# Loading one input in 640-byte runs by four narrow loads, with heads paired g and g+4, in a chunked linear-attention kernel

## The chip, the cores and the metric

One core of one Trainium2 chip (the sets of runs were taken on several chips, each with the kernel before in the same rounds). The metric is device microseconds of one execution. A time quoted below is the median of all runs of a kernel, of which up to two are marked slow (over 1.5% above its fastest run); a ratio is of fast runs alone.

The engines go by their short names: PE is TensorE (matmuls and transposes), ACT ScalarE, DVE VectorE, POOL GpSimd. SP is SyncE, which here computes nothing and issues DMA transfers; SPq is its queue. To issue a load is the instruction that starts it; the 16 DMA engines then move it in packets, one for each contiguous run. An eviction copies a result of PE out of its accumulation buffer. The chain of waits is followed back from the last instruction: at each step to what it had waited for.

## The reference

An RWKV-7-like recurrence, then a mixing layer. Only the first part touches the change.

```python
# r, k, v, w, a, b: (batch 4, heads 8, seq 768, head_dim 40), float32
for t in range(S):
    y[:, :, t] = einsum('bhd,bhde->bhe', rt, state)
    Sa = einsum('bhde,bhe->bhd', state, at)
    state = state * wt[:, :, None, :] - einsum('bhd,bhe->bhde', Sa, bt) + einsum('bhd,bhe->bhde', vt, kt)
# then x = y as (batch, seq, 320):  theta = x @ w_theta;  y = w_tok_r @ (x cos theta) + w_tok_i @ (x sin theta)
# u = x + y;  out = u + relu(u @ w_ch)
```

## The kernel before

The sequence is cut in 24 tiles of 128 time steps (6 for each batch entry). For a tile the six inputs are loaded with time on the partitions: each partition gets 8 heads x 40 floats, which lie 8 x 160 bytes apart in memory, so one 160 KB load is 1024 runs of 160 bytes. Pairs of heads are then transposed on PE and evicted by ACT.

```python
def load(i):                                    # cut: r and v share a buffer
    def src(ap):
        return ap[bi, :, ci * C:(ci + 1) * C, :].rearrange("h t d -> t h d")
    return (..., (("raw_r", s), raw_rv[s][:, 0], src(r)),
                 (("raw_v", s), raw_rv[s][:, 1], src(v)))

def loads(i):
    for key, dst, src in load(i):
        add("SP", "load", i, lambda dst=dst, src=src: nc.sync.dma_start(out=dst, in_=src),
            650, [], [key], work=1030)
...
# in prep(i): r and v copied to bf16 (POOL), 8 transposes (PE), one eviction (ACT)
tr("trv", "erv", (rv[:, 0], rv[:, 1]), rvT_t[i % (NTR + 1)], ...)
```

`add` does not emit at once. It records an operation with an estimated cost, and a planner then fixes the order of all operations on every engine from these costs and from priorities (`OFF`, `TIMES`), found by search. Each engine runs its list strictly in that order. All loads go through SP's queue. For them the planner keeps one clock of DMA work, and lets SP run ahead of it by a fixed time:

```python
SP_DEPTH = 3600.0
te = max(te, dma - SP_DEPTH)            # SP may issue when DMA work ahead is under 3.6 us
free[o.eng] = t + o.cost                # then SP is busy for `cost` ...
dma = max(dma, t + 1350.0) + o.work     # ... and the DMA engines for `work`
```

## Time and profile before

| | before |
|---|---|
| time, median of the first 4 runs | 219.81 us (219.03 to 221.12) |
| PE busy | 197.0 us of a span of 217.5 us |
| DVE, ACT, POOL busy | 166.0, 146.9, 118.4 us |
| loads: packets of 160 bytes | 147,456 of 155,684 |

From the page of the kernel before: PE's busy row of part 1; busy tenths in 40 slices of the span; DMA packets; the main queue; the chain of waits.

```profile
span 217.5 us, 8118 instructions
...
PE 197.0 (91%) x3368; PEld 155.8 (72%) x3368; DVE 166.0 (76%) x250; ACT 146.9 (68%) x319; POOL 118.4 (54%) x184
...
PE   1487898888898899999999999999999999999993
...
PEclk9999999999999999999999999999999999999999
DMA  6998989989998999999978999899897010101022
...
DMA packets 155684, 30.81 MB, mean 142 GB/s; under 512 B 150400, under 2 KB 155648, under 8 KB 155648
...
q1 hardware_dynamic: 153216, 27.54, 70.3%
...
PE 71%; DVE 10%; DMA 7%; POOL 4%; issue 4%; ACT 2%; SPq 1%; POOLq 0%; DVEq 0%; ACTq 0%
PE ps_s L685 19%; PE ps_s L396 14%; PE ps_d L484 9%; PE ps_s L631 8%; DMA raw_a<-in_a_dram 4%; PE ps_s L588 4%; DVE lamu L489 3%; DMA wrow_i<-in_moe_w_tok_i_dram 3%; PE ps_s L617 2%; DVE phi L489 2%; PE ps_s L536 2%; POOL kb L452 2%; DVE psi L489 2%; PE ps_s L554 2%; PE ps_s L524 2%
```

The DMA row stands at 7 to 9 until three quarters of the span, and the PE row stays at 9 only from slice 15 on.

The same in stretches of 20 us (columns: busy us and instruction count of each engine, granted clock, DMA share, GB/s):

```profile
core 0: us, PE busy (x) PEld busy (x) DVE busy (x) ACT busy (x) POOL busy (x), PEclk, DMA share, GB/s
20.00:40.00 20.00, 17.30 (x335) 13.54 (x335) 15.54 (x17) 13.19 (x33) 12.22 (x19) 1.00 1.00 163
40.00:60.00 20.00, 16.84 (x322) 13.12 (x322) 15.49 (x19) 15.59 (x32) 14.55 (x22) 1.00 0.98 170
60.00:80.00 20.00, 17.84 (x349) 14.80 (x347) 15.66 (x20) 15.54 (x33) 14.48 (x23) 1.00 1.03 174
```

PE has 2 to 3 us of slack in each 20 us, while the DMA share is 0.98 to 1.03. Who waits for loads, in total us, times, longest:

```profile
engine line waited for: us in total, times, longest us
...
POOL kb L452 <- DMA raw_rv<-in_v_dram: 4.0, 2, 2.5
...
ACT lw L423 <- DMA raw_w<-in_w_dram: 1.5, 1, 1.5
...
DVE ah L456 <- DMA raw_a<-in_a_dram: 1.2, 1, 1.2
```

With two waits of 0.3 us that are not shown, 7.3 us in six waits. By the timeline ACT's and DVE's lie in the first 8 us, and POOL's two (put down to a load of v) at 127 and 160 us.

I also use a measure of my own, worked out from the instruction times in the trace. Every matmul is priced at its back-to-back spacing in the timeline (135 ns for 320 columns, 55 for 128, 35 for 80, 25 for 40 or fewer, 28 in the 64-row score groups), plus 107 ns (estimate) for each change between 64- and 128-row work; "lost" is the time at which a tile's first matmul starts, less the price of all matmuls before it. In the kernel before 26.3 us are lost when the 11th tile starts (78.3 us) and 29.3 us at the 24th (172.5 us). So the first 80 us hold nearly all of PE's slack up to there.

### The profile page before, as it was taken

The page shows a single profiled execution, that of the slowest core. Times are in us where ns is not written, and L with a number is a line of the kernel's source. Part 1 is how long each engine was busy: PE and PEld are TensorE (multiplying, and loading weights), DVE is VectorE, ACT ScalarE, POOL GpSimd, SP SyncE. Part 2 cuts the span into 40 slices and gives each one's busy share as a digit, 9 for nine tenths or more (in the row PEclk, how much of TensorE's full clock was granted, in tenths as well). Part 3 has the DMA queues.
Part 4 walks back from the last instruction along what each step waited for, and adds up shares of the span by engine and source line. Part 5 has one row for each costly group of instructions (what it writes and reads, how often), then busy time and mean ns, then how long its engine had stood idle before and what let it go on. Part 6 is the DMA issues. An engine that isn't in the chain of part 4 may idle for free.

```text
span 217.5 us, 8118 instructions
## 1 busy us (share of the span) xinstructions
PE 197.0 (91%) x3368; PEld 155.8 (72%) x3368; DVE 166.0 (76%) x250; ACT 146.9 (68%) x319; POOL 118.4 (54%) x184
## 2 busy tenths in 40 slices
PE   1487898888898899999999999999999999999993
PEld 1375667657677678688787778878787888777771
DVE  7468678875989758888999668888979978866533
ACT  4356675977679769978559956899599864863111
POOL 5000688298673992894762972697658660165000
PEclk9999999999999999999999999999999999999999
DMA  6998989989998999999978999899897010101022
GB/s 108 194 183 148 175 145 168 179 152 169 171 189 140 178 175 187 183 202 178 184 137 160 153 192 161 162 187 156 149 211 123 33 63 5 60 33 60 33 90 90
DMA packets 155684, 30.81 MB, mean 142 GB/s; under 512 B 150400, under 2 KB 155648, under 8 KB 155648
## 3 DMA queue, kind: packets, MB, share of 16 engines
q1 hardware_dynamic: 153216, 27.54, 70.3%
q0 software_dynamic: 2432, 2.77, 7.8%
q8 instruction: 26, 0.43, 0.8%
q14 instruction: 10, 0.08, 0.1%
HBM read 29.13 MB, written 3.93 MB: 152 GB/s over the span
## 4 chain that ended last, share of the span: by engine, by line
PE 71%; DVE 10%; DMA 7%; POOL 4%; issue 4%; ACT 2%; SPq 1%; POOLq 0%; DVEq 0%; ACTq 0%
PE ps_s L685 19%; PE ps_s L396 14%; PE ps_d L484 9%; PE ps_s L631 8%; DMA raw_a<-in_a_dram 4%; PE ps_s L588 4%; DVE lamu L489 3%; DMA wrow_i<-in_moe_w_tok_i_dram 3%; PE ps_s L617 2%; DVE phi L489 2%; PE ps_s L536 2%; POOL kb L452 2%; DVE psi L489 2%; PE ps_s L554 2%; PE ps_s L524 2%
## 5 line engine op out<-in xcount | busy, mean ns | idle before, releaser
L452 POOL TENSOR_TENSOR kb<-raw_kb,ex 128x320 bf16<-128x320 f32 x44 | 37.4, 862 | 18.1 <-ACT ex L445 12.5
L685 PE MATMUL ps_s<-zr,wtok_r 128*128 128x320 bf16 x144 | 40.9, 300 | 0.2 <-ACT gd L572 0.2
L685 PE MATMUL ps_s<-zi,wtok_i 128*128 128x320 bf16 x144 | 40.8, 299 | 0.0
L489 DVE TENSOR_TENSOR psi<-ps_d,mask_p 128x1024 bf16<-128x1024 f32 x24 | 29.3, 1222 | 9.3 <-PE ps_d L484 9.2
L456 POOL TENSOR_TENSOR ah<-raw_a,ex 128x320 bf16<-128x320 f32 x22 | 18.9, 861 | 28.2 <-ACT ex L445 23.0
L489 DVE TENSOR_TENSOR lamv<-ps_d,mask_p 128x1024 bf16<-128x1024 f32 x24 | 29.1, 1219 | 6.2 <-PE ps_d L484 6.1
L667 POOL TENSOR_TENSOR zr<-cs,x 128x320 bf16<-128x320 f32 x23 | 17.8, 793 | 28.7 <-ACT cs L655 28.7
L489 DVE TENSOR_TENSOR lamu<-ps_d,mask_p 128x1024 bf16<-128x1024 f32 x24 | 29.0, 1219 | 4.6 <-PE ps_d L484 4.3
L489 DVE TENSOR_TENSOR phi<-ps_d,mask_n 128x1024 bf16<-128x1024 f32 x24 | 29.1, 1217 | 0.8 <-PE ps_d L484 0.7
L445 ACT ACTIVATE ex<-ps_d 128x656 f32<-128x656 f32 x24 | 17.2, 719 | 7.4 <-PE ps_d L440 6.4
L461 POOL CAST rv<-raw_rv 128x320 bf16<-128x320 f32 x44 | 18.6, 451 | 0.0
L399 ACT COPY kbT<-ps_s 128x512 f32<-128x512 f32 x24 | 14.1, 588 | 6.1 <-PE ps_s L396 5.7
L484 PE MATMUL ps_d<-aT,kbT 64*128 64x128 bf16 x384 | 16.8, 221 | 1.5 <-ACT ex L445 0.7
L695 DVE TENSOR_TENSOR u<-ps_s,x 128x320 bf16<-128x320 f32 x24 | 11.7, 488 | 8.1 <-PE ps_s L685 7.9
L667 POOL TENSOR_TENSOR zi<-cs,x 128x320 bf16<-128x320 f32 x23 | 17.8, 794 | 0.0
L399 ACT COPY uT<-ps_s 128x192 f32<-128x192 f32 x24 | 7.5, 320 | 14.8 <-PE ps_s L588 14.8
L685 PEld LDWEIGHTS <-wtok_r 128*128 128x128 bf16 x144 | 14.0, 97 | 4.6
L396 PE MATMUL ps_s<-ident,kb 128*128 128x128 bf16 x192 | 15.7, 223 | 1.7 <-DVE kb L452 1.3
L685 PEld LDWEIGHTS <-wtok_i 128*128 128x128 bf16 x144 | 14.1, 98 | 4.1 <-issue 0.4
L624 DVE TENSOR_TENSOR x<-ps_s,ex 128x320 bf16<-128x320 f32 x24 | 11.7, 487 | 6.3 <-PE ps_s L617 5.5
L617 PE MATMUL ps_s<-kb,lamu 128*128 128x40 bf16 x192 | 15.0, 180 | 1.3 <-DVE lamu L489 1.2
L399 ACT COPY rvT<-ps_s 128x512 f32<-128x512 f32 x24 | 14.2, 593 | 2.7 <-PE ps_s L396 2.5
(109 smaller groups left out, 547.1 us busy)
## 6 DMA issues: line engine op xcount, KB each, us to landing
raw_w<-in_w_dram SPq DMA_DIRECT2D x24, 160.0 KB, 3.9
raw_kb<-in_k_dram SPq DMA_DIRECT2D x24, 160.0 KB, 3.9
raw_kb<-in_b_dram SPq DMA_DIRECT2D x24, 160.0 KB, 3.6
raw_a<-in_a_dram SPq DMA_DIRECT2D x24, 160.0 KB, 4.3
raw_rv<-in_r_dram SPq DMA_DIRECT2D x24, 160.0 KB, 4.2
raw_rv<-in_v_dram SPq DMA_DIRECT2D x24, 160.0 KB, 4.2
out_dram<-oo SPq DMA_DIRECT2D x24, 160.0 KB, 1.8
wrow_r<-in_moe_w_tok_r_dram POOLq DMA_DIRECT2D x6, 192.0 KB, 4.8
```

The lines of the kernel that those rows point to most:

```text
L396: nc.tensor.transpose(out=dst[:, c:c + 128], in_=pair(src, g), identity=ident)
L399: nc.scalar.copy(out=out.bitcast(FP32), in_=in_)
L445: add("ACT", "exp", i, lambda: nc.scalar.activation(out=ex, in_=ps(pk)[:, :, 0:328], func=AF.Exp), 717, [pk], [kex], table="lnexp")
L452: lambda j=j: (nc.vector if fast else nc.gpsimd).tensor_tensor(out=kb[:, j, :, 0:D], in0=raw_kb[s4][:, j], in1=invW, op=ALU.mult),
L456: lambda: (nc.vector if fast else nc.gpsimd).tensor_tensor(out=ah[:, :, 0:D], in0=raw_a[s4], in1=Wi, op=ALU.mult),
L461: lambda j=j: (nc.scalar.copy if fast else nc.gpsimd.tensor_copy)(out=rv[:, j, :, 0:D], in_=raw_rv[s4][:, j]),
L484: nc.tensor.matmul(t[:, q, g, :], lhsT=lhs[rows(q), g * 128:(g + 1) * 128], rhs=rhs[rows(q), g * 128:(g + 1) * 128], start=True, stop=True)
L489: add("DVE", kindm, i, lambda: nc.vector.tensor_tensor(out=dst.rearrange("p a b c -> p (a b) c"), in0=ps(p).rearrange("p a (g c) -> p (a g ...
L617: nc.tensor.matmul(o, lhsT=lamu[:, p, g, :], rhs=kb[:, 1, h, 0:D], start=False, stop=True, skip_group_check=True)
L631: nc.tensor.matmul(dst, lhsT=lhs[:, kt, :], rhs=rhs[:, kt, :], start=kt == 0, stop=kt == 2)
L667: nc.vector if fast else nc.gpsimd).tensor_tensor(
L685: nc.tensor.matmul(ps(pk)[:, 0:DM], lhsT=wtok[nm][:, s, j * 128:(j + 1) * 128], rhs=zs[c][:, s], start=n == 0 and c == 0, stop=n == NT - 1 ...
```

## The change

Its intent is to lessen DMA work. Four consecutive time steps of one head are 640 contiguous bytes. If a partition holds four time steps of two heads, r of a tile is 256 runs of 640 bytes in place of 1024 of 160. A partition is then a pair (group of heads g, time step group t), which is not one stride in memory, so the load is cut in four of 32 partitions. r is transposed in four pieces (one for each of the four steps), and the eviction puts the time steps back in order; so r and v are evicted apart. The heads of a pair become g and g+4. The priorities were searched anew.

```diff
+        rr = r[bi, :, ci * C:(ci + 1) * C, :].rearrange("(c g) (t q) d -> g t c (q d)", c=2, q=4)
...
-                (("raw_r", s), raw_rv[s][:, 0], src(r)),
-                (("raw_v", s), raw_rv[s][:, 1], src(v)))
+                [("raw_v", s), raw_v[s], src(v)],
+                *([("raw_r", s, g), raw_r[s][32 * g:32 * g + 32], rr[g]] for g in range(G)))
...
+            small = key[0] == "raw_r"
+            add("SP", "loadr" if small else "load", i,
+                lambda dst=dst, src=src: nc.sync.dma_start(out=dst, in_=src),
+                350 if small else 650, [], [key], work=110 if small else 1030)
...
-        tr("trv", "erv", (rv[:, 0], rv[:, 1]), rvT_t[i % (NTR + 1)], ...
+        tr("tv", "ev", (vb,), vT_t[i % NTR], [("v", i % NRV)], ("vT", i % NTR), "ACT")
+            for q in range(4):
+                nc.tensor.transpose(out=t[:, q * 128:q * 128 + 128],
+                                    in_=rb[:, q].rearrange("p c d -> p (c d)"), identity=ident)
+        add("ACT", "er", i, lambda: nc.scalar.copy(
+            out=rT.rearrange("p (g t q) -> p g t q", g=G, q=4),
+            in_=ps(pr).bitcast(BF16)[:, 0:512].rearrange("p (q g t) -> p g t q", q=4, g=G)),
+            592, [pr], [("rT", i % (NTR + 1))])
... (all of OFF, WAIT, TSWITCH and TIMES; the pairing in k, b, a, v and x; one 8-column matmul per tile removed)
```

More of the change, by code (lines that the diff above doesn't have):

```diff
@@ L231 @@
 OFF = dict(
-    ah=-29.76, ch=42.32, cs=-23.68, ea=-5.68, egd=-64.18, egt=9.05, ekb=-1.05, enu=-33.25,
-    enut=-26.71, erv=-11.79, eth=-30.49, eut=-42.87, ewt=25.44, ex=-7.68, exp=-112.65,
-    ext=9.87, gd=25.41, gt=10.89, kb=6.58, ln=-1.17, load=-12.1, mlu=70.45, mlv=15.71,
-    mphi=35.75, mpsi=75.19, nu=-16.23, nut=3.78, nx=-57.27, oo=43, row=42.66, rv=9.85,
-    sin=53.93, slu=-3.56, slv=6.28, sphi=-11.65, spsi=-15.12, st=42.29, ta=1.92, th=30.73,
-    tkb=-0.04, trv=-1.76, uadd=20.68, ut=30.15, wdma=56, wt=28.14, x0=-37.84, xt=23.63,
-    y=-16.87, z=-2.05)
-WAIT, TSWITCH = 416.01, 546374.0
+    ah=-26.07, ch=33.52, cs=-21.39, ea=-40.38, egd=-92.25, egt=-8.68, ekb=9.63, enu=-58.5,
+    enut=-23.31, er=-5.46, eth=-38.45, eut=-55.9, ev=5.12, ewt=19.8, ex=-41.21, exp=-57.89,
+    ext=-20.87, gd=20.28, gt=17.91, kb=21.44, ln=-9.62, load=-20.29, loadr=-17.17, mlu=40.67,
+    mlv=35.18, mphi=17.24, mpsi=78.31, nu=-19.89, nut=-5.64, nx=-102.69, oo=31.37, r=11.38,
+    row=34.5, sin=45.81, slu=-9.57, slv=12.56, sphi=-24.11, spsi=-25.79, st=39.12, ta=8.91,
+    th=30.76, tkb=5.84, tr=5.27, tv=-1.08, uadd=13.1, ut=29.99, v=-27.53, wdma=76.67, wt=36.01,
+    x0=-26.11, xt=28.7, y=-17.83, z=-15.67)
+WAIT, TSWITCH = 385.43, 116473.0
 TIMES = dict(
     tile=[
-        -39.53, -34.24, -29.51, -3.78, 20.04, 41.89, 38.94, 51.03, 56.49, 58.19, 71.7, 90.01,
-        94.38, 97.37, 114.43, 121.89, 126.37, 125.37, 126.65, 137.15, 152.75, 154.06, 155.36,
-        173.39],
+        -71.09, -61.56, -58.38, -27.55, 3.72, 30.71, 27.6, 47.5, 47.98, 54.51, 66.55, 83.21,
+        91.62, 95.2, 113.45, 119.12, 120.48, 131.71, 131.96, 138.38, 147.11, 149.87, 154.28,
+        165.27],
     row=[
-        51.82, 57.24, 68.97, 70.44, 94.9, 101.27, 93.77, 118.11, 124.13, 107.33, 127.65,
-        140.22, 116.14, 132.99, 161.62, 121.8, 167.43, 194.51, 178.51, 189.99, 186.39, 240.98,
-        241.1, 195.27],
+        43.61, 52.41, 50.75, 69.75, 80.59, 88.92, 81.97, 112.09, 121.2, 111.03, 132.7, 140.28,
+        132.9, 146.81, 158.14, 143.14, 159.03, 151.07, 189.54, 198.88, 168.12, 226.39, 228.51,
+        212.32],
     rel=[
-        -29.38, 28.51, 59.76, 33.74, 24.97, 97.39, 29.98, 104.9])
+        -34.49, 18.1, 55.63, 38.99, 11.12, 98.01, -12.6, 104.7])
 @with_exitstack
@@ L289 @@
     raw_kb = sb("raw_kb", [128, 2, H, D], FP32, 4)
-    raw_rv = sb("raw_rv", [128, 2, H, D], FP32, 4)
+    raw_v = sb("raw_v", [128, H, D], FP32, 4)
+    raw_r = sb("raw_r", [128, 2, 4 * D], FP32, 4)
     def load(i):
         bi, ci = divmod(i, NCH)
+        s = i % 4
         def src(ap):
             return ap[bi, :, ci * C:(ci + 1) * C, :].rearrange("h t d -> t h d")
-        s = i % 4
-        return ((("raw_w", s), raw_w[s], src(w)),
-                (("raw_k", s), raw_kb[s][:, 0], src(k)),
-                (("raw_b", s), raw_kb[s][:, 1], src(b)),
-                (("raw_a", s), raw_a[s], src(a)),
-                (("raw_r", s), raw_rv[s][:, 0], src(r)),
-                (("raw_v", s), raw_rv[s][:, 1], src(v)))
+        rr = r[bi, :, ci * C:(ci + 1) * C, :].rearrange("(c g) (t q) d -> g t c (q d)", c=2, q=4)
+        return ([("raw_w", s), raw_w[s], src(w)],
+                [("raw_k", s), raw_kb[s][:, 0], src(k)],
+                [("raw_b", s), raw_kb[s][:, 1], src(b)],
+                [("raw_a", s), raw_a[s], src(a)],
+                [("raw_v", s), raw_v[s], src(v)],
+                *([("raw_r", s, g), raw_r[s][32 * g:32 * g + 32], rr[g]] for g in range(G)))
     ident = consts.tile([128, 128], BF16, name="ident")
@@ L337 @@
     kb_t = padded("kb", [128, 2, H, 64], NKB, last24)
-    rv_t = padded("rv", [128, 2, H, 64], NRV, last24)
+    v_t = padded("v", [128, H, 64], NRV, last24)
+    r_t = padded("r", [128, 4, 2, 64], 2, last24)
     nu_t = padded("nu", [128, H, 64], 2, last24)
@@ L349 @@
     nc.vector.memset(wch[:, 2, :], 0.0)
-    ex_t = sb("ex", [128, 2, 328], FP32, NEX)
+    ex_t = sb("ex", [128, 2 * DM + 8], FP32, NEX)
     aT_t = sb("aT", [128, 512], BF16, NTR)
     kbT_t = sb("kbT", [128, 1024], BF16, NTR)
-    rvT_t = sb("rvT", [128, 1024], BF16, NTR + 1)
+    rT_t = sb("rT", [128, 512], BF16, NTR + 1)
+    vT_t = sb("vT", [128, 512], BF16, NTR)
     nuT_t = sb("nuT", [128, 512], BF16, 2)
@@ L413, in loads, with natural, paired @@
         for key, dst, src in load(i):
-            add("SP", "load", i, lambda dst=dst, src=src: nc.sync.dma_start(out=dst, in_=src),
-                650, [], [key], work=1030)
+            small = key[0] == "raw_r"
+            add("SP", "loadr" if small else "load", i,
+                lambda dst=dst, src=src: nc.sync.dma_start(out=dst, in_=src),
+                350 if small else 650, [], [key], work=110 if small else 1030)
+    def natural(t):
+        return t.rearrange("p (c g) d -> p g c d", c=2)
+    def paired(t):
+        return t.rearrange("p (g c) d -> p g c d", c=2)
     def prep(i):
@@ L420, in prep @@
         ex = ex_t[i % NEX]
-        kb, rv, ah = kb_t[i % NKB], rv_t[i % NRV], ah_t[i % 3]
+        kb, vb, ah = kb_t[i % NKB], v_t[i % NRV], ah_t[i % 3]
+        rb = r_t[i % 2]
         kex = ("ex", i % NEX)
         add("ACT", "ln", i, lambda: nc.scalar.activation(
-            out=lw[:, :, 0:D], in_=raw_w[s4], func=AF.Ln), 473,
+            out=paired(lw)[:, :, :, 0:D], in_=natural(raw_w[s4]), func=AF.Ln), 473,
             [("raw_w", s4)], [("lw", s2)], table="lnexp")
@@ L429, in cs @@
             t = ps(pk)
-            nc.tensor.matmul(t[:, 0, 0:DM], lhsT=ntri_inc, rhs=lw[:, :, 0:D],
+            nc.tensor.matmul(t[:, 0, 512 - DM:512], lhsT=ntri_inc, rhs=lw[:, :, 0:D],
                              start=True, stop=True)
@@ L439, in cs @@
                                  rhs=ones2, start=False, stop=True, skip_group_check=True)
-            nc.tensor.matmul(t[:, 0, DM:DM + 8], lhsT=ident,
-                             rhs=off_diag.rearrange("p g c -> p (g c)"),
-                             start=True, stop=True, skip_group_check=True)
-        add("PE", "cs", i, cs, 2 * mm(320) + 6 * 25, [("lw", s2)], [pk], new=(pk, 2),
-            tail=tail(8))
+        add("PE", "cs", i, cs, 2 * mm(320) + 5 * 25, [("lw", s2)], [pk], new=(pk, 2),
+            tail=tail(2))
         add("ACT", "exp", i, lambda: nc.scalar.activation(
-            out=ex, in_=ps(pk)[:, :, 0:328], func=AF.Exp), 717, [pk], [kex], table="lnexp")
-        invW = ex[:, 0, 0:DM].rearrange("p (h d) -> p h d", h=H)
-        Wi = ex[:, 1, 0:DM].rearrange("p (h d) -> p h d", h=H)
+            out=ex, in_=ps(pk).rearrange("p a b -> p (a b)")[:, 512 - DM:512 + DM + 8],
+            func=AF.Exp), 710, [pk], [kex], table="lnexp")
+        invW = ex[:, 0:DM].rearrange("p (g c d) -> p g c d", g=G, c=2)
+        Wi = ex[:, DM:2 * DM].rearrange("p (g c d) -> p g c d", g=G, c=2)
         fast = i < 2
@@ L452, in prep @@
                 lambda j=j: (nc.vector if fast else nc.gpsimd).tensor_tensor(
-                    out=kb[:, j, :, 0:D], in0=raw_kb[s4][:, j], in1=invW, op=ALU.mult),
+                    out=paired(kb[:, j])[:, :, :, 0:D], in0=natural(raw_kb[s4][:, j]), in1=invW, op=ALU.mult),
                 490 if fast else 864, [("raw_" + nm, s4), kex], [("kb", j, i % NKB)])
@@ L456, in prep @@
             lambda: (nc.vector if fast else nc.gpsimd).tensor_tensor(
-                out=ah[:, :, 0:D], in0=raw_a[s4], in1=Wi, op=ALU.mult),
+                out=paired(ah)[:, :, :, 0:D], in0=natural(raw_a[s4]), in1=Wi, op=ALU.mult),
             490 if fast else 864, [("raw_a", s4), kex], [("ah", i % 3)])
-        for j, nm in enumerate("rv"):
-            add("ACT" if fast else "POOL", "rv", i,
-                lambda j=j: (nc.scalar.copy if fast else nc.gpsimd.tensor_copy)(
-                    out=rv[:, j, :, 0:D], in_=raw_rv[s4][:, j]),
-                460, [("raw_" + nm, s4)], [("rv", j, i % NRV)])
+        copy = nc.scalar.copy if fast else nc.gpsimd.tensor_copy
+        add("ACT" if fast else "POOL", "v", i,
+            lambda: copy(out=paired(vb)[:, :, :, 0:D], in_=natural(raw_v[s4])),
+            460, [("raw_v", s4)], [("v", i % NRV)])
+        add("ACT" if fast else "POOL", "r", i,
+            lambda: copy(out=rb[:, :, :, 0:D],
+                         in_=raw_r[s4].rearrange("p c (q d) -> p q c d", q=4)),
+            460, [("raw_r", s4, g) for g in range(G)], [("r", i % 2)])
         def tr(kind, kinde, srcs, dst, skeys, dkey, eng):
@@ L473, in prep, with tr_r @@
         tr("ta", "ea", (ah,), aT_t[i % NTR], [("ah", i % 3)], ("aT", i % NTR), "ACT")
-        tr("trv", "erv", (rv[:, 0], rv[:, 1]), rvT_t[i % (NTR + 1)],
-           [("rv", 0, i % NRV), ("rv", 1, i % NRV)], ("rvT", i % (NTR + 1)), "ACT")
+        tr("tv", "ev", (vb,), vT_t[i % NTR], [("v", i % NRV)], ("vT", i % NTR), "ACT")
+        pr = ("ps", "tr", i)
+        def tr_r():
+            t = ps(pr).bitcast(BF16)
+            for q in range(4):
+                nc.tensor.transpose(out=t[:, q * 128:q * 128 + 128],
+                                    in_=rb[:, q].rearrange("p c d -> p (c d)"), identity=ident)
+        add("PE", "tr", i, tr_r, 4 * mm(128), [("r", i % 2)], [pr], new=(pr, 1), tail=tail(128))
+        rT = rT_t[i % (NTR + 1)]
+        add("ACT", "er", i, lambda: nc.scalar.copy(
+            out=rT.rearrange("p (g t q) -> p g t q", g=G, q=4),
+            in_=ps(pr).bitcast(BF16)[:, 0:512].rearrange("p (q g t) -> p g t q", q=4, g=G)),
+            592, [pr], [("rT", i % (NTR + 1))])
     def scores(i, kind, kindm, lhs, rhs, keys, dst, dkey, mask):
@@ L495, in attention_scores @@
         st, s2 = i % NTR, i % NSC
-        kbT, aT, rvT = kbT_t[st], aT_t[st], rvT_t[i % (NTR + 1)]
+        kbT, aT, vT, rT = kbT_t[st], aT_t[st], vT_t[st], rT_t[i % (NTR + 1)]
         scores(i, "spsi", "mpsi", kbT[:, 0:512], aT, [("kbT", st), ("aT", st)],
@@ L500, in attention_scores @@
                phi_t[s2], ("phi", s2), mask_n)
-        scores(i, "slv", "mlv", rvT[:, 512:], rvT[:, 0:512], [("rvT", i % (NTR + 1))],
+        scores(i, "slv", "mlv", vT, rT, [("vT", st), ("rT", i % (NTR + 1))],
                lamv_t[s2], ("lamv", s2), mask_p)
@@ L506, in recurrence @@
         st, s2 = i % NTR, i % 2
-        aT, kb, rv = aT_t[st], kb_t[i % NKB], rv_t[i % NRV]
+        aT, kb, vb = aT_t[st], kb_t[i % NKB], v_t[i % NRV]
         psi, phi = psi_t[i % NSC], phi_t[i % NSC]
@@ L510, in recurrence @@
         gt_old, gt_new = gt_t[(i + 1) % 2], gt_t[i % 2]
-        vb = rv[:, 1]
         pk = ("ps", "x0", i)
@@ L527, in recurrence @@
         add("PE", "x0", i, x0, 8 * 25 + (0 if first else 4 * mm(80)),
-            [("aT", st), ("psi", i % NSC), ("rv", 1, i % NRV)] +
+            [("aT", st), ("psi", i % NSC), ("v", i % NRV)] +
             ([] if first else [("gt", (i + 1) % 2)]), [pk], new=(pk, 1), tail=tail(40))
@@ L558, in recurrence @@
             add("PE", "gt", i, gt_mm, 8 * mm(80) + (0 if first else mm(320)),
-                [("kb", 0, i % NKB), ("kb", 1, i % NKB), ("rv", 1, i % NRV), ("nu", s2)] +
+                [("kb", 0, i % NKB), ("kb", 1, i % NKB), ("v", i % NRV), ("nu", s2)] +
                 ([] if first else [("gt", (i + 1) % 2)]), [gk], new=(gk, 1), tail=tail(80))
-            wm = ex_t[i % NEX][:, 1, DM:DM + 8].rearrange("p (n o) -> p n o", o=1)
+            wm = ex_t[i % NEX][:, 2 * DM:2 * DM + 8].rearrange("p (n o) -> p n o", o=1)
             add("DVE", "egt", i, lambda: nc.vector.tensor_tensor(
@@ L596, in readout @@
         s2, srv = i % NSC, i % (NTR + 1)
-        rvT, kb = rvT_t[srv], kb_t[i % NKB]
-        scores(i, "slu", "mlu", nuT_t[i % 2], rvT[:, 0:512],
-               [("nuT", i % 2), ("rvT", srv)], lamu_t[s2], ("lamu", s2), mask_p)
+        rT, kb = rT_t[srv], kb_t[i % NKB]
+        scores(i, "slu", "mlu", nuT_t[i % 2], rT,
+               [("nuT", i % 2), ("rT", srv)], lamu_t[s2], ("lamu", s2), mask_p)
         lamv, lamu = lamv_t[s2], lamu_t[s2]
@@ L608, in y @@
                     nc.tensor.matmul(t[:, g * 80:g * 80 + 80],
-                                     lhsT=rvT[:, g * 128:(g + 1) * 128],
+                                     lhsT=rT[:, g * 128:(g + 1) * 128],
                                      rhs=gd[:, 2 * g:2 * g + 2, :], start=True,
@@ L619, in readout @@
         add("PE", "y", i, y, 16 * 25 + (0 if first else 4 * mm(80)),
-            [("rvT", srv), ("lamv", s2), ("lamu", s2), ("kb", 0, i % NKB),
+            [("rT", srv), ("lamv", s2), ("lamu", s2), ("kb", 0, i % NKB),
              ("kb", 1, i % NKB)] + ([] if first else [("gd", (i + 1) % 2)]), [pk],
@@ L624, in readout @@
         add("DVE", "ex", i, lambda: nc.vector.tensor_tensor(
-            out=x[:, 0:DM], in0=ps(pk)[:, 0:DM], in1=ex_t[i % NEX][:, 1, 0:DM],
+            out=x[:, 0:DM].rearrange("p (c g d) -> p g c d", c=2, g=G),
+            in0=ps(pk)[:, 0:DM].rearrange("p (g c d) -> p g c d", c=2, g=G),
+            in1=ex_t[i % NEX][:, DM:2 * DM].rearrange("p (g c d) -> p g c d", c=2, g=G),
             op=ALU.mult), 488, [pk, ("ex", i % NEX)], [("x", i % NX)])
```

## The prediction

> **What bounds the kernel now.** Two limits in turn.
>
> 1. To about 80 us, DMA. The stretch table gives a DMA share of 0.92 to 1.09 per 10 us, with PE busy 8.1 to 9.6 of 10 us. Of 155,684 packets 147,456 are 160-byte runs; in the packet records one takes 15.2 ns, so a 160 KB load (1024 packets on 16 engines) costs 0.97 us, a tile's six 5.8 us. The Trainium skill, "DMA: Bandwidth & Descriptors", section Specifications, asks for at least 512 B per transfer for line rate; the trace agrees: 160 B in 15.2 ns, 1280 B (stores) in 60 ns, twice the rate.
> 2. After 80 us, PE: busy 9.8 to 10.0 of 10 us, and the chain of waits is nearly all PE. In the timeline matmuls start back to back: 135 ns for 320 columns, 55 for 128, 35 for 80, 25 for 40.
>
> I priced every matmul with these spacings plus 107 ns (estimate) per change between 64- and 128-row work (124 changes): 184 us of the span of 217.5. PE has lost 26.3 us against this price when the 11th tile's first matmul starts (78.3 us), and only 3 us more up to the 24th (172.5 us). Of the 26.3, 13.5 go before the 3rd tile, the rest at 1.6 us per tile while loads are slow. Only the first ~80 us can be shortened.
>
> **What the change does.**
> - r: 256 packets of 640 B per tile for 1024. A line through the medians at 160 B (14 ns) and 1280 B (55 ns) gives 32 ns (estimate): 0.51 us per tile for 0.97. Saved: 0.46 us per tile, 11 us in all.
> - SP: 72 more issues; at 0.35 to 0.5 us each about +1 us per tile, hidden while issues already stretch to 0.97 us each behind full DMA.
> - PE: one 8-column matmul fewer per tile (0.6 us in all); as many transposes. 126 mode changes. Priced total 183.3.
> - ACT: an rvT eviction of 593 ns becomes vT (~380, as aT) and a strided rT (~590, estimate): 9 us in all. ACT is 68% busy: off the path, but some latency returns.
> - POOL, DVE: the same elements with one more dimension; the same times.
> - Priorities: up to the 13th tile as many mix matmuls (36) precede it as before; afterwards tiles go first (120 of 288 mix matmuls before the 24th tile, were 152). PE is full there: that moves work without shortening it.
>
> **On the critical path.** Only tiles loaded while PE is short of work: 11 x 0.46 = 5 us, plus up to 0.6 from PE, minus about 0.5 of ACT latency. 219.6 - 5 = about 214.3. The other 6 us of saved DMA fall where PE is full and buy nothing.
>
> **Predicted: 214.3 us, 8 in 10 between 210.8 and 217.8.** Faster by over 2%: 0.63; within 2%: 0.34; slower by over 2%: 0.03.
>
> **What would show it.** 640-byte packets near 32 ns; DMA busy total down by 11 us, loads ending about 10 us earlier; PE's 11th tile 4 to 6 us earlier, lost time there near 21 us; the distance from there to the end within 1.5 us of before; rT eviction 550 to 650 ns; POOL's multiplies near 862 ns.
>
> **What would make it wrong.** 640-byte packets into 32 partitions cost 50 ns or more; SP's nine issues per tile become the limit; POOL slows with the deeper access pattern; before 80 us a chain through ACT, DVE and POOL rather than DMA sets the pace (no gain); or the new order cuts stalls by more than the loads explain (more gain).

## The result, and the profile after

The changed kernel takes 231.12 us (229.03 to 231.96, 4 runs) against 219.81 us. The ratio is 1.0494, with a 95% interval of 1.0407 to 1.0581: slower by 5%. Ratios here and below are the mean time of one kernel's fast runs over that of the kernel before in the same rounds, so not quite the ratio of the medians.

The same lines of the page after:

```profile
span 230.2 us, 8200 instructions
...
PE 200.4 (87%) x3344; PEld 159.0 (69%) x3344; DVE 166.8 (72%) x252; ACT 151.2 (66%) x341; POOL 119.5 (52%) x184
...
PE   1587988888775999999699999799969999999993
...
PEclk9999999999999999999979999999979999999999
DMA  7996897979989897988799794879678200110222
...
DMA packets 138406, 30.83 MB, mean 134 GB/s; under 512 B 126976, under 2 KB 138368, under 8 KB 138368
...
q1 hardware_dynamic: 135936, 27.54, 62.3%
...
PE 56%; DMA 13%; SPq 11%; issue 6%; ACT 5%; POOL 5%; DVE 3%; ACTq 0%; POOLq 0%; DVEq 0%
PE ps_s L712 16%; SPq L420 11%; PE ps_s L400 8%; PE ps_s L658 7%; PE ps_d L510 7%; DMA raw_w<-in_w_dram 5%; PE ps_s L613 3%; DMA raw_v<-in_v_dram 3%; DMA raw_r<-in_r_dram 2%; PE ps_s L494 2%; DMA raw_a<-in_a_dram 2%; POOL kb L463 2%; PE ps_s L642 1%; PE ps_s L579 1%; PE ps_s L640 1%
```

There are fewer packets (138,406) and the main queue's share is down, 70.3% to 62.3%: the DMA engines have less to do. Yet the loading goes on longer (the DMA row falls to 0 with slice 33, which begins at 32/40 of 230.2 us, 184 us; before with slice 32, at 31/40 of 217.5 us, 169 us), the PE row still has slices of 6 and 7 behind its 15th, and in the chain of waits SP's queue, SPq, has grown from 1% to 11% and DMA from 7% to 13%. (SPq's share alone is no proof: it is 6% in the one-issue kernel below, which is faster than the kernel before.) The clock row shows two slices below 9.

```profile
core 0: us, PE busy (x) PEld busy (x) DVE busy (x) ACT busy (x) POOL busy (x), PEclk, DMA share, GB/s
20.00:40.00 20.00, 16.86 (x308) 12.98 (x308) 14.56 (x15) 13.33 (x33) 9.91 (x15) 1.00 0.78 142
40.00:60.00 20.00, 17.44 (x349) 14.15 (x349) 16.52 (x20) 16.92 (x38) 14.88 (x23) 1.00 0.95 161
60.00:80.00 20.00, 14.89 (x298) 12.08 (x295) 14.24 (x16) 14.67 (x32) 13.12 (x21) 1.00 0.89 155
```

In 20 to 40 and 60 to 80 us the DMA share is 0.78 and 0.89: the DMA engines go idle where they were full before, and PE, DVE and POOL do less. The waits for loads:

```profile
engine line waited for: us in total, times, longest us
...
ACT lw L436 <- DMA raw_w<-in_w_dram: 9.9, 7, 2.5
POOL v L472 <- DMA raw_v<-in_v_dram: 9.0, 5, 3.4
POOL r L475 <- DMA raw_r<-in_r_dram: 8.1, 6, 1.9
...
POOL ah L467 <- DMA raw_a<-in_a_dram: 6.7, 2, 5.7
```

What was 1.5 us in one wait is 9.9 us in seven for w, and POOL waits 23.8 us in 13 waits for v, r and a, where it waited 4.0 us in two. With DVE's single wait it is 34.8 us in 21 waits, for 7.3 us in six before. By the measure of lost time, 29.6 us are lost when the 11th tile starts (82.5 us) and 42.0 us at the 24th (177.3 us), where it was 26.3 and 29.3: most of the loss falls after the 11th tile, in the part that was full of PE work before. One stretch of the chain of waits (start us, us, what):

```profile
107.17 2.06 SPq L420
...
109.27 1.66 SPq L420
...
110.97 0.43 SPq L420
...
111.44 0.42 SPq L420
...
111.91 1.59 SPq L420
...
113.60 2.83 DMA raw_w<-in_w_dram
...
116.51 0.12 ACT lw L436
```

For 6.3 us on end the chain is SP issuing: v 2.06 us, then the four loads of r, which begin at 109.27, 110.97, 111.44 and 111.91 us; only then can the next tile's w be issued, which lands 2.8 us later, and ACT's `lw` follows it at once. In that time PE stands still (start us, us, instruction; in brackets the idle time before it):

```profile
111.41 0.30 PE L712 MATMUL ps_s<-zi,wtok_i 128*128 128x320 bf16 x1
113.78 0.40 PE L400 MATMUL ps_s<-ident,v 128*128 128x128 bf16 x4 [2.07 <-POOL v L472]
```

At 114.3 us, just after that wait of 2.07 us, the clock record shows PE at half speed for 3.4 us, and once more at 168.9 us, after a wait of PE of 2.19 us; the kernel before has no such stretch before its end.

### The profile page after: what moved, and what is told of

Same layout as the page of the kernel before. It is cut to its first block, busy times and chain, and to the rows that moved or that the text cites. A ratio compares the mean times of both kernels' runs of the same rounds, so it can differ in the third digit from the quotient of the medians.

```text
span 230.2 us, 8200 instructions
## 1 busy us (share of the span) xinstructions
PE 200.4 (87%) x3344; PEld 159.0 (69%) x3344; DVE 166.8 (72%) x252; ACT 151.2 (66%) x341; POOL 119.5 (52%) x184
## 2 busy tenths in 40 slices
DMA packets 138406, 30.83 MB, mean 134 GB/s; under 512 B 126976, under 2 KB 138368, under 8 KB 138368
## 3 DMA queue, kind: packets, MB, share of 16 engines
q1 hardware_dynamic: 135936, 27.54, 62.3%
## 4 chain that ended last, share of the span: by engine, by line
PE 56%; DMA 13%; SPq 11%; issue 6%; ACT 5%; POOL 5%; DVE 3%; ACTq 0%; POOLq 0%; DVEq 0%
PE ps_s L712 16%; SPq L420 11%; PE ps_s L400 8%; PE ps_s L658 7%; PE ps_d L510 7%; DMA raw_w<-in_w_dram 5%; PE ps_s L613 3%; DMA raw_v<-in_v_dram 3%; DMA raw_r<-in_r_dram 2%; PE ps_s L494 2%; DMA raw_a<-in_a_dram 2%; POOL kb L463 2%; PE ps_s L642 1%; PE ps_s L579 1%; PE ps_s L640 1%
## 5 line engine op out<-in xcount | busy, mean ns | idle before, releaser
L467 POOL TENSOR_TENSOR ah<-raw_a,ex 128x320 bf16<-128x320 f32 x22 | 19.0, 862 | 41.4 <-ACT ex L455 32.1
L515 DVE TENSOR_TENSOR lamu<-ps_d,mask_p 128x1024 bf16<-128x1024 f32 x24 | 29.3, 1220 | 6.9 <-PE ps_d L510 6.2
L515 DVE TENSOR_TENSOR psi<-ps_d,mask_p 128x1024 bf16<-128x1024 f32 x24 | 29.3, 1220 | 4.9 <-PE ps_d L510 4.2
L455 ACT ACTIVATE ex<-ps_d 128x648 f32<-128x648 f32 x24 | 17.1, 713 | 9.7 <-PE ps_d L451 5.5
L510 PE MATMUL ps_d<-aT,kbT 64*128 64x128 bf16 x384 | 17.4, 221 | 1.6 <-DVE lamu L515 0.8
L436 ACT ACTIVATE lw<-raw_w 128x320 bf16<-128x320 f32 x24 | 11.4, 476 | 10.0 <-DMA raw_w<-in_w_dram 9.9
L640 PE MATMUL ps_s<-kb,lamv 128*128 128x40 bf16 x192 | 15.5, 181 | 2.2 <-ACT nuT L403 2.2
L587 DVE TENSOR_TENSOR gt<-ps_s,ex 128x320 bf16<-128x320 f32 x20 | 9.8, 488 | 9.7 <-ACT rT L498 6.0
L498 ACT COPY rT<-ps_s 128x512 bf16<-128x512 bf16 x24 | 14.2, 595 | 3.4 <-PE ps_s L494 3.1
```

Of the source, the lines that this page charges most:

```text
L455: add("ACT", "exp", i, lambda: nc.scalar.activation(out=ex, in_=ps(pk).rearrange("p a b -> p (a b)")[:, 512 - DM:512 + DM + 8], func=AF.Ex ...
L467: lambda: (nc.vector if fast else nc.gpsimd).tensor_tensor(out=paired(ah)[:, :, :, 0:D], in0=natural(raw_a[s4]), in1=Wi, op=ALU.mult),
L498: add("ACT", "er", i, lambda: nc.scalar.copy(out=rT.rearrange("p (g t q) -> p g t q", g=G, q=4), in_=ps(pr).bitcast(BF16)[:, 0:512].rearra ...
L510: nc.tensor.matmul(t[:, q, g, :], lhsT=lhs[rows(q), g * 128:(g + 1) * 128], rhs=rhs[rows(q), g * 128:(g + 1) * 128], start=True, stop=True)
L515: add("DVE", kindm, i, lambda: nc.vector.tensor_tensor(out=dst.rearrange("p a b c -> p (a b) c"), in0=ps(p).rearrange("p a (g c) -> p (a g ...
L640: nc.tensor.matmul(o, lhsT=lamv[:, p, g, :], rhs=kb[:, 0, h, 0:D], start=first, stop=False, skip_group_check=True)
```

## The experiments

The theory to test (A): each load takes SP about 0.4 us or more to issue, whatever it carries; four small ones carry only 0.5 us of DMA work together, so the queue drains while they are issued and the next tile's large loads come late. Rivals: (B) the new order is worse by itself; (C) packets of 640 bytes into 32 partitions are slow. I compared the built instruction lists: except for the two kernels that move r's loads to another queue, and the repair that failed, every variant below has exactly the order of its parent on PE, DVE, ACT and POOL (the order in the traces says the same). Kernels that are wrong read r from the wrong places, or not at all, with the same work on every compute engine.

### How many issues: one, two, four, eight

To load the same 256 runs of 640 bytes in one issue, r is read as a flat array with a single partition stride. The data are wrong, the traffic is the same.

```diff
-        rr = r[bi, :, ci * C:(ci + 1) * C, :].rearrange("(c g) (t q) d -> g t c (q d)", c=2, q=4)
+        rr = r[bi].rearrange("h t d -> (h t d)").rearrange("(c n p x) -> n p c x", c=2, n=NCH, p=128)[ci]
-                *([("raw_r", s, g), raw_r[s][32 * g:32 * g + 32], rr[g]] for g in range(G)))
+                # g = 0 loads raw_r[s] whole; g = 1, 2, 3 emit nothing (or: g = 0, 2 load 64 partitions each)
```

> The changed kernel with its plan untouched, every compute engine's order identical; r comes as one 128-partition load of the same 256 runs of 640 B per tile, in place of four 32-partition loads. It reads the right amount from the wrong places of r, so the result is wrong on purpose. Theory A (the loading queue is limited by issues: each small issue takes at least 0.42 us and brings only 0.13 us of DMA work, so the DMA engines run dry): the loss vanishes, total 213 to 219 us, last load issued before 162 us. Rival B (the new order of instructions and priorities is worse by itself): 229 to 232 us. Rival C (640-byte packets are slow, 40 ns in the mean): packet mean stays near 40 ns and time near 230 us.

> As the one-issue kernel, but two loads of 64 partitions each per tile (result wrong on purpose). Theory A: between the one-issue kernel and the changed kernel, 215 to 224 us. Rivals B and C: no change from 231 us.

For eight, each of the four loads is cut in two of 16 partitions; the result is correct.

> The changed kernel with each of the four loads of r split in two of 16 partitions: same bytes, same packets, eight issues per tile; result correct. Theory A: four more issues at 0.42 us or more make 1.7 us per tile, up to 40 us over 24 tiles, of which a part is hidden: 250 to 272 us. Rivals B and C: within 3 us of 231 us.

| issues of r per tile | median us | ratio to the kernel before (95%) |
|---|---|---|
| 1 (wrong) | 216.05 | 0.9852 (0.9802 to 0.9901) |
| 2 (wrong) | 220.15 | 1.0053 (0.9991 to 1.0114) |
| 4 (the changed kernel) | 231.12 | 1.0494 (1.0407 to 1.0581) |
| 8 (correct) | 272.49 | 1.2471 (1.2393 to 1.2548) |

The same bytes in the same packets, the same order everywhere: 56 us between one issue and eight (the last 0.5 us above my range, the others inside). From one to two, an added issue costs 4.1 us / 24 = 0.17 us; from two to four 11.0 / 48 = 0.23 us; from four to eight 41.4 / 96 = 0.43 us. The last is about what SP needs for one (columns: duration ns min/median/max, first and last start). The changed kernel, then eight issues:

```profile
L420 SPq DMA_DIRECT2D raw_r<-in_r_dram x96: 312/427/1971, 4.5 to 177.2; - x96
```

```profile
L423 SPq DMA_DIRECT2D raw_r<-in_r_dram x192: 312/422/1961, 4.3 to 216.3; - x192
```

The medians are 427 and 422 ns. As long as SP has spare time an added issue is partly hidden; at eight, hardly anything hides it.

SP's own account supports this: summed over the traces, its issues up to the last load take 139.2 us with one issue of r, 152.5 with two, 161.7 with four and 196.1 with eight, and the last load is issued at 158.0, 165.2, 177.2 and 216.3 us. From one to eight that is 56.9 us more of issuing, a last load 58.3 us later, and 56.4 us more time. That the slope meets the median issue so closely is partly luck: long issues bring the mean of r's in the eight-issue kernel to 0.52 us, and PE ran at half clock there for 47.8 us in all, which can cost up to 24 us of PE's work, where it was 6.8 us with four issues and none with one or two.

Rival B falls: the same order takes 216.05 us with one issue. Last load before 162 us was expected too, and holds (158.0). Rival C falls too: in the one-issue kernel a 640-byte packet still takes 39 ns in the mean (40 in the changed kernel, median 32 in both), and the time is 15 us less.

### The kernel before, with r in four

```diff
+                n = 32 if key[0] == "raw_r" else 128
+                for p in range(0, 128, n):
+                    nc.sync.dma_start(out=dst[p:p + n], in_=src[p:p + n])
```

> The kernel before with its one load of r cut into four loads of 32 partitions, each 256 runs of 160 B; result correct, order of all compute engines as before. A quarter brings 0.24 us of DMA work for an issue of at least 0.42 us. Theory A: slower than before by 2 to 6 per cent (224 to 233 us), with the DMA share falling in the first 160 us. Rivals B and C: within 1 per cent of 219.8 us, as neither order nor packet size changes.

224.2 us, ratio 1.0217 (1.0171 to 1.0262), correct. Four issues hurt the old order too, with the old packets, at the lower edge of my range (one of the four runs was slow; the fast ones have a median of 223.8). The loss is smaller than in the changed kernel. A likely reason, not tested, is that a quarter of r here brings 256 packets and keeps the DMA engines busy for 0.24 us, nearly twice as long.

### Three empty issues

The one-issue kernel, plus three loads per tile of 32 partitions by 32 bytes into a scratch tile.

```diff
+    tiny = sb("tiny", [128, 8], FP32, 4)
+                # g = 0: raw_r[s] whole;  g = 1, 2, 3: tiny[s][32g:32g+32] <- rr[32g:32g+32, 0, 0:8]
```

> The one-issue kernel (216.05 us; r read from the wrong places, so wrong on purpose) with three more loads per tile of 32 partitions by 32 bytes into a scratch tile nobody reads: the same four issues as the changed kernel at the same places, but all of r's bytes in the first. Theory A (the number of issues on SP's queue costs, whatever they carry): 226 to 234 us. Rival F (loads narrowed to 32 partitions, or four completions that r's consumer must wait for, cost): 216 to 219 us.

231.94 us, ratio 1.0533 (1.0480 to 1.0586): the changed kernel's time again, although all of r came in one piece and the three loads carry 3 KB. Only its chain of waits is shown, and no time is read from it.

```profile
span 232.0 us, 8168 instructions
...
PE 52%; SPq 18%; DMA 10%; ACT 7%; issue 7%; POOL 4%; DVE 1%; ACTq 0%; POOLq 0%; DVEq 0%
SPq L425 18%; PE ps_s L718 15%; PE ps_s L403 8%; PE ps_s L664 7%; DMA raw_w<-in_w_dram 7%; PE ps_d L516 6%; PE ps_s L619 3%; DMA raw_a<-in_a_dram 2%; POOL kb L469 1%; PE ps_s L585 1%; PE ps_s L500 1%; POOL ah L473 1%; PE ps_s L648 1%; PE ps_s L567 1%; DMA tiny<-in_r_dram 1%
```

SPq is 18% of that chain. So it is the number of issues on SP's queue that costs, not that r's own bytes come by narrow loads, nor their packets; rival F falls, and r's consumer hardly waited for the empty loads (0.4 us once). The empty loads are narrow themselves. That what an issue costs is SP's time, and not something else that each issue brings, rests on SP's account above, as moving the issues (below) gave no clean test.

### Packet size, with one issue

```diff
+                # g = 0: one load, src(r), 1024 runs of 160 bytes, into raw_r[s];  g = 1, 2, 3 emit nothing
```

> The changed kernel, its plan and every compute engine's order untouched, with r in one issue again and in the old 1024 runs of 160 B per tile (laid down in the wrong order, so the result is wrong on purpose). It isolates packet size at one issue: against the one-issue kernel with 640-byte runs (216.05 us) it has 0.46 us more DMA work per tile. If the larger packets are worth what I predicted, it takes 3 to 6 us more, 219 to 222 us. If the gain of the one-issue kernel comes from the new order alone, it takes 215 to 217 us.

217.52 us, ratio 0.9896 (0.9851 to 0.9941). Against the one-issue kernel with 640-byte runs (216.05 us, 0.9852) the old packets cost about 1.5 us by the medians and 0.4% by the ratios; as the intervals overlap, this is an estimate and could be nothing. It lies far under the 5 us that I had predicted. The time fell between my two ranges (215 to 217, and 219 to 222 us), in neither. The rest of the gain, about 1%, is there with the old packets: it belongs to what else changed, the new order with its pairing, with r and v evicted apart and with one small matmul fewer per tile. These were not separated.

### Taking r's traffic away

If DMA volume had set the pace of the first 80 us, taking away r's loads would have to show. Both kernels load r for four tiles only.

```diff
+                if key[0] != "raw_r" or i < 4:
                     nc.sync.dma_start(out=dst, in_=src)
```

> The kernel before, r loaded for the first four tiles only; the result is wrong on purpose. From tile 5 on it takes away 0.97 us of DMA work and one issue per tile, twice what 640-byte runs would save. My prediction's step (DMA sets the pace to 80 us, each 0.46 us saved per tile before the 11th comes off the time) says 0.97 x 7 = 6.8 us faster, about 213 us. Theory D, if it holds for the kernel before too: under 2 us faster, 217.5 to 219.8 us.

> The one-issue kernel (plan and compute order of the changed kernel) with r loaded for the first four tiles only; later tiles use stale r, so the result is wrong on purpose. It takes away another 0.6 us of DMA work and one issue per tile from tile 5 on. Theory D (in the plan of the changed kernel, once r takes one issue, compute dependences and not DMA set the pace of the first 80 us, which is why 640-byte packets bought only about 1 us): within 1.5 us of the one-issue kernel's 216.05 us, and SP waits longer for buffers. Rival E (DMA volume still sets that pace, as my prediction said): 4 to 5 us faster, 210 to 212.5 us.

The kernel before without r: 219.4 us, ratio 0.9992 (0.9944 to 1.0039). Nothing, for 3.3 MB less. Its stretches:

```profile
core 0: us, PE busy (x) PEld busy (x) DVE busy (x) ACT busy (x) POOL busy (x), PEclk, DMA share, GB/s
20.00:40.00 20.00, 17.26 (x334) 13.54 (x335) 15.54 (x17) 13.23 (x33) 12.22 (x19) 1.00 1.01 165
40.00:60.00 20.00, 16.83 (x323) 13.17 (x323) 15.48 (x19) 15.59 (x32) 14.60 (x22) 1.00 0.94 160
60.00:80.00 20.00, 17.88 (x347) 14.74 (x347) 15.60 (x20) 15.57 (x33) 14.53 (x23) 1.00 1.04 174
```

To be read against those of the kernel before: PE 17.26, 16.83 and 17.88 us, there 17.30, 16.84 and 17.84; the DMA share is 1.01, 0.94 and 1.04, still full, because the loads run further ahead: the 11th tile's w lands 12.5 us before its use, where it was 6.6 us. (In the changed kernel, w of 9 of the 24 tiles lands 0.1 us or less before its use; in the kernel before that is so for the first tile alone.) Its 11th tile starts on PE at 78.2 us (before: 78.3) and its 24th at 172.4 us (172.5).

The one-issue kernel without r: 215.91 us, ratio 0.9828 (0.9781 to 0.9875), against 216.05 us and 0.9852 with it. Rival E falls in both plans, and the half of theory D that says DMA volume does not set the pace holds; that dependences among the compute engines do is not shown by this.

### Moving r's loads to another queue

`nc.sync` becomes `nc.scalar`, or `nc.gpsimd`, for the loads of r in the changed kernel; both are correct.

> The changed kernel with only the four loads of r moved from SP's queue to ACT's, at the same places in the plan; result correct. If what hurts is issue time on SP's queue, SP has five issues per tile again and its share of the chain of waits goes away; ACT pays for 96 issues, at 0.4 us each up to 40 us on an engine that is 66 per cent busy. Theory A: faster than the changed kernel by at least 5 us, 214 to 226 us. If instead small loads hurt wherever they are issued (in the DMA engines): within 3 us of 231 us.

> The changed kernel with only the four loads of r moved from SP's queue to POOL's; result correct. POOL pays about 0.55 us for each of 96 issues (as its other loads do), 53 us on an engine that is 52 per cent busy, so some of its multiplies come late. Theory A: 216 to 228 us, SP's share of the chain gone. If small loads hurt wherever they are issued: within 3 us of 231 us.

247.68 us (ratio 1.1295, 1.1210 to 1.1381) on ACT's queue, and 247.22 us (1.1264, 1.1196 to 1.1332) on POOL's. Both expectations were missed. They do not test theory A cleanly, because they bring a new wait: a load now stands in the list of a compute engine, behind compute work that waits for other things. On POOL each of the 96 also occupies the engine:

```profile
L420 POOL DMA_DIRECT2D raw_r<-in_r_dram x96: 537/547/604, 5.4 to 192.4; - x96
```

which is 0.55 us x 96 = 53 us. And SP, with fewer issues, is not quicker, since its list has output stores in it and these wait for results that are late. SP's wait for `oo`, first on the kernel before, then with r on ACT's queue:

```profile
SPq L707 <- DVE oo L704: 47.6, 15, 7.8
```

```profile
SPq L734 <- DVE oo L731: 82.2, 17, 10.3
```

While SP waits there, the loads behind it are not issued: with r on ACT's queue SP issues none from 87.7 to 111.9 us, and from 95 to 105 us the DMA share is 0.20. The total alone proves nothing, though: the kernel before without r has 65.0 us of this wait and loses no time. I did not separate the shares of these two effects.

### A repair that failed: r of three tiles in one load

From the kernel before, with new priorities from a search of mine in the kernel's planner: 384 time steps as 128 partitions x 3 steps, one load of 1024 runs of 480 bytes for three tiles.

```diff
+        src = r[bi, :, n * C:(n + 3) * C, :].rearrange("h (p q) d -> p h (q d)", q=3)
+                out=rT_t[j % 2].rearrange("x g (p q) -> x g p q", q=3)[:, :, :, q],   # eviction, every third element
```

> A repair meant to beat both, result correct: from the kernel before, r for three tiles (384 time steps) in one load of 128 partitions, three consecutive time steps in each partition, 1024 runs of 480 B. That is one issue and some 0.55 us of DMA work per tile (estimate, on the line through 160 and 1280 B) in a third of an issue per tile. Transposed per tile as before and put in time order by the strided eviction; heads paired as before; priorities searched with the kernel's own planner. Theory A expects no SP share above that of the kernel before and 213 to 217.5 us. If the extra copies and evictions (ACT 9 us more) or the new priorities eat it: 218 us or more.

225.97 us, ratio 1.0281 (1.0238 to 1.0324), correct. One issue in three tiles did not help, and SPq's share of the chain, 5%, is above the 1% of the kernel before, against my expectation. Another cost was added, which may be a reason: its eviction writes every third bf16, and takes 1060 ns where the changed kernel's, which reads with a stride and writes contiguously, takes 595 (busy us, mean ns):

```profile
line engine op names shapes xcount | busy us, mean ns | idle before us <-releasers
L441 ACT COPY rT<-ps_s 128x512 bf16<-128x512 bf16 x24 | 23.0, 1060 | 0.4 <-PE ps_s L401 0.4
```

```profile
L498 ACT COPY rT<-ps_s 128x512 bf16<-128x512 bf16 x24 | 14.2, 595 | 3.4 <-PE ps_s L494 3.1
```

That is 23.0 us of ACT in place of 14.2 us. Whether the rest of its loss comes from my priorities was not tested.

### A version that beats both

The plan and order of the changed kernel, with r loaded in one issue of 160-byte runs, and transposed and evicted like v.

```diff
-                *([("raw_r", s, g), raw_r[s][32 * g:32 * g + 32], rr[g]] for g in range(G)))
+                *([("raw_r", s, g), raw_r[s], src(r) if g == 0 else None] for g in range(G)))
-            for q in range(4):
-                nc.tensor.transpose(... rb[:, q] ...)
+            transpose_pairs(ps(pr).bitcast(BF16), (rb,))
+        add("ACT", "er", i, lambda: copy_words(rT, ps(pr)[:, 0:256]), ...)
```

> A version meant to beat both, result correct: the changed kernel's plan and order on every engine (pairs g with g+4, v and r evicted apart, new priorities), but r loaded as before, in one issue of 160-byte runs, transposed and evicted like v. The shorter eviction (about 380 ns for 595) is the only other difference. As removing r's traffic from the kernel before bought nothing, DMA volume should not matter: 216 to 218 us, ratio to the kernel before 0.98 to 0.992, all of it from the new order. If the gain of the wrong-on-purpose one-issue kernels was an artefact: 219 us or more.

217.29 us (216.36 to 217.80), ratio 0.9878 (0.9840 to 0.9916), correct. It keeps the change's order and drops its loads: 1.2% faster than the kernel before (the interval leaves out 1) and some 6% faster than the changed one.

## Why the prediction was wrong

Two steps failed, one of them with the wrong sign.

1. **"SP: 72 more issues; ... about +1 us per tile, hidden while issues already stretch to 0.97 us each behind full DMA."** This is the step that turned a gain into a loss. The count was 3 more for each of 24 tiles, as stated, but they were only half hidden. The 96 issues of r took 58.7 us of SP (0.61 us in the mean) where 24 had taken 20.9 us: 1.6 us more per tile, not 1. The other loads' issues did give way, from 118.8 to 99.7 us in all (0.99 to 0.83 us in the mean), but that hides 19.1 of the 37.8 us, no more; the last load was issued at 177.2 us, after 163.7 before. The small loads are what empties the queue: one brings 64 packets x 32 ns / 16 engines = 0.13 us of work and takes SP 0.43 us. Going from one issue to four costs 15 us (216.05 to 231.12 us), and three empty issues cost the same. The late loads also undid my second limit, that PE is full after 80 us: from the 11th tile's start to the end I had allowed a change of 1.5 us, and it grew from 139.2 to 147.7 us. I had named the limit under "what would make it wrong", but had compared SP's time for a tile with the tile's time, 1 us more out of 7, where I should have asked how long the queue lasts while SP sends nothing of weight. The author's planner makes the same error: it counts 350 ns for such an issue and lets SP run ahead by a fixed 3.6 us.
2. **"Only tiles loaded while PE is short of work: 11 x 0.46 = 5 us."** Packets of 640 bytes do take 32 ns in the median, but 40 in the mean. I had set the mean of 160-byte packets (15.2 ns) against a median, so that r's work fell by 0.33 us per tile, not 0.46; the packets' time on 16 engines fell from 172.0 to 163.8 us, 8 us and not 11. The work saved is real, but the time did not depend on it. In the kernel before, taking r away altogether gave a ratio of 0.9992. I had read "DMA share 1.0 and PE not full" as "DMA sets the pace". The list of waits showed hardly any waiting for loads between 10 and 80 us, and the chain 7% of DMA; had I trusted these, this term would have been near 0. What does set the pace of 7.1 us per tile (3rd to 11th tile, 21.2 to 78.3 us, over 8) where PE's price is 5.5 us, I did not settle; dependences between PE, ACT, DVE and POOL in a fixed order remain the likely cause, but that is argued only.

What held: only the first 80 us had something to give (though the rest had something to lose). In the kernel with one issue and old packets the 11th tile finds 23.7 us lost, where the kernel before had 26.3, and its 24th 26.8 against 29.3: the new order's gain lies before the 11th tile. The eviction of rT took 595 ns (I had said 550 to 650) and POOL's multiplies 864 ns (862 before). What I did not foresee was that the new order by itself was worth 1%.

Summed up by the medians, from 219.8 us: the new order about -2 us, larger packets about -1.5 us or nothing, four issues in place of one +15 us, which gives 231. (These are steps along one row of kernels, so that they add up is no check.) Part of the 15 us may be PE's halved clock after waits: two stretches of 3.4 us can cost at most 3.4 us of full-speed work together, as in each of them half the speed is lost.

## What to carry to other kernels

Count what a queue earns by an issue: here a load brought 0.13 us of DMA work for 0.43 us of issuing, the queue drained, and the large loads behind came late; fewer packets did not make up for that. A DMA share near 1 does not say that loads limit the time: here it stayed at 0.94 to 1.04 with r's loads gone, and the time was the same. Whether loads limit anything is read from who waits for a load, or tested by removing one. Do not set a mean against a median when sizing a saving. When a change brings both a new layout and a new search of priorities, try the new order with the old layout: here that was the only part worth keeping.

## What the Trainium skill lacked or had wrong

- "DMA: Bandwidth & Descriptors", Issuing engines are not separate DMA queues: it says that issuing on several engines saves only the sequencer's time, "which is usually small relative to the DMA itself". Here that time was 0.43 us for 0.13 us of DMA work, and it decided the result. Moving those issues to ACT's or POOL's queue gave 247.7 and 247.2 us, in place of 231.1; the page does not say that a load there waits for its turn behind compute work.
- "DMA: Bandwidth & Descriptors", Rules for kernel authors: it advises one 128-partition transfer in place of two to disjoint halves, as both share the same engines. The advice is right (216.05, 220.15, 231.12 and 272.49 us for one, two, four and eight), but the reason that the runs show is issuing; with three empty loads the loss was the same (ratio 1.0533). No section gives an issue time measured on this chip, or one that depends on the width (there is a cycle count for earlier generations, beside another chip's): here 422 to 427 ns in the median for 16 and 32 partitions, 606 ns for 64, 747 ns for 128 in the one-issue kernel.
- "DMA: Bandwidth & Descriptors", Specifications: at least 512 B for line rate. No step at 512 B was seen here in the medians: packets took 14 ns at 160 B, 26 at 480, 32 at 640 and, for stores, 55 to 58 at 1280 (58 in the kernel before, 55 in the changed one).
- "TensorE: Matmul & The Clock Gate", Part 1: it puts the fall to half clock after an idle window of about 3.4 us. Here PE waits of 2.07 and 2.19 us were each followed by a half-speed stretch of 3.4 us, with PE busy for 1.35 and 1.22 us of the 3.4 us before the fall; the length agrees, the idle time was shorter.
- No page gives a time for a strided write by ACT (strides are treated only in general): 1060 ns for 512 bf16 elements with every third written, against 595 ns with a strided read and a contiguous write.
- Not settled, and on no page: single issues of over 1.15 us, up to 4.1 us, are scattered over every trace. In the changed kernel 4 of the 11 issues of r longer than 1.15 us start within 0.15 us of a 16 KB packet on the instruction queue, the other 7 do not; no run tested it. They are part of what r's issues cost there (0.61 us in the mean for a median of 0.43).
